# Head dimensions in neighbouring pairs across the partitions, fillers over the whole wait, a later planned landing

## The chip, the cores and the metric

The kernel runs on one core of a Trainium2 chip. The metric is device time in microseconds (us); the version before the change takes 1041.48 us, the median of three runs (1041.34 to 1042.71). Below, PE is the matrix engine (its weight loads are listed apart, as PEld), DVE the vector engine, ACT the scalar engine, POOL the GpSimd engine, and SP the engine whose queue issues the DMAs.

## What is computed

Four layers over a sequence of 2048 tokens of width 576 in bf16: attention, GLU, attention, GLU, each with a layer norm in front and a residual behind it. The two attention layers share their weights, and so do the two GLU layers.

```
x = x + A(layernorm(x))     # attention
x = x + B(layernorm(x))     # GLU
x = x + A(layernorm(x))
x = x + B(layernorm(x))

A: q, k, v = (x @ wqkv) as (3, 32 heads, 18 dims)
   logits[s, w] = q[s] . k[s - 2w] * 18**-0.5   for w = 0..7, -1e9 where s - 2w < 0
   o[s] = sum over w of softmax(logits)[s, w] * v[s - 2w];  return o @ wo
B: return ((x @ w_gate) * (x @ w_up)) @ w_down      # inner width 4608
```

Each token looks at eight earlier positions, two apart, in 32 heads of 18 dimensions. The attention is thus small products and sums on the vector engine, and nearly all matmul work is in the GLU.

## The kernel before, in words

**Tiles and stages.** The sequence is cut into tiles of 256 tokens (the first two of the first layer of 128). For each tile `attention` and then `glu` are called; j counts these stages. The sequence goes in two halves of eight 128-token blocks, each first through layer pair one and then through pair two. The GLU keeps its gate and up weights in SBUF and streams the down weights.

**The planner.** No call issues its work at once. Every piece is given to `Plan.op` (L48) with an engine, an assumed cost in ns, the names that it reads and writes, a priority and a rank (the stage, mostly; lower is more urgent). `Plan.run` (L109) keeps a clock for each engine, takes the piece that can begin first, and emits the pieces in that order. So the assumed costs and landing times decide the order of the instructions on each engine, and each engine then runs its own list strictly in order. For a DMA, the assumed end is a modelled transfer plus 2000 ns plus `late`. A piece of lower rank that would soon be ready holds back longer pieces of higher rank on its engine (L154 to L160).

**Fillers.** Until the first GLU piece, the planner puts dummy matmuls (L1207 to L1209, into an unused bank) into waits of PE. Their number is worked out at L176 to L179 from the gap between the clock of PE and the start of the next real piece. Pieces with a cost of zero, which emit nothing, move that clock too. One of them, at L884, holds a bank for the first gather until the attention weights have been spread.

**The head layout.** The weights arrive with columns ordered (head, dim), 18 dims to a head. The kernel copies them into `wqkv` with columns ordered (dim, head), so that after the projection the partitions of a 128-row block hold four dims of 32 heads: partition 32 * dim + head. The copies are made in `perm` (L388 to L418) for each of five 128-row slabs k, and for t3 = 0 (Q), 1 (K), 2 (V, in two halves), 3 (dims 16 and 17 of Q and K) and 4 (those of V). Each reads its source with a step of 18 elements. Q and the Q/K tails go to DVE; K goes to DVE for odd k and to ACT for even k; the V halves go to whichever of ACT and DVE the planner finds free first; the V tails go to ACT. The raw Q/K weights are loaded at L364 in six DMAs (slab 4 in two parts); the V loads wait until slab 2 of Q/K has landed.

**The first tile.** For j = 0 (`fast`) everything is ordered for a short chain: layer norm (L467 on), transposes of the normalised rows (L524), projection slab by slab as weights become ready (L606), products of q with the eight shifted k on DVE (L761), sums over the dims by the selector matrix `Esel` on PE (L776), softmax (L802 to L827), attention weights spread over the dims by the selectors `Bsel` (L842) and copied out of PSUM, products with v (L875), their sum by identity matmuls, the gathers (L879, L880), scaling (L902, L905), output projection (L940), residual (L910), the next layer norm, and the first GLU matmul (L993).

**Later tiles.** From j = 3 on, the attention weights are written to DRAM (L852) and read back by four DMAs (L855), one for each dim of four, each to 32 partitions. The first product with v (L875) waits for them. The planner assumes `late=1200` for these reads. GLU results are taken out of PSUM by ACT (L1028) and DVE (L1035), which frees the banks for PE.

## Time and profile before

| What | us |
|---|---|
| median of three runs | 1041.48 |
| lowest and highest run | 1041.34, 1042.71 |
| the profiled execution, in all | 1043.98 |
| its span, from first to last instruction | 1041.8 |
| PE busy in it | 1030.0 (99%) |
| DVE busy in it | 774.4 (74%) |
| ACT busy in it | 436.9 (42%) |

A page of the profile and answers about its trace are quoted below. In the windows by stage, each row is a stretch of time with its length, then the busy time of PE, PEld, DVE, ACT and POOL with the number of instructions, the granted PE clock (1.00 is full), the share of the DMA engines' time, and GB/s. In the order of time, a row has the start, how long the merged instructions lasted, engine, line, operation, what was written and read, the count, and in brackets the idle time just before with what ended it. In the rows grouped by line and form, busy time and the mean ns of one instruction stand behind the bar. In the waits, a row has the waiting engine and line, what it waited for, the us in total, the times, and the longest.

### The profile page before, as it was taken

Reading aid. Unit: us, or ns where it says so; the run is one execution under the profiler, and the core shown is the slowest. Engines: PE = TensorE matmul, PEld = TensorE weight load, DVE = VectorE, ACT = ScalarE, POOL = GpSimd, SP = SyncE. Lnnn points to the kernel's source line nnn. Section 1 sums busy time; section 2 is a strip of 40 time slices with the busy share of each in tenths; the row PEclk is TensorE's granted clock in tenths of the full one; section 3 lists DMA queues with packets and bytes.
Section 4 is the critical chain, followed back from the end, with each engine's and each line's share of the span. In section 5 each row is a group of like instructions: output and inputs, shape, how many; then the busy total and the mean of one; then the engine's idle time right before and its main releaser. Section 6 shows DMA issues by size and latency. Waiting matters only on the chain.

```text
span 1041.8 us, 40082 instructions
## 1 busy us (share of the span) xinstructions
PE 1030.0 (99%) x17899; PEld 813.5 (78%) x17899; DVE 774.4 (74%) x1450; ACT 436.9 (42%) x1169; POOL 8.9 (1%) x33
## 2 busy tenths in 40 slices
PE   7999999999999999999999999999999999999998
PEld 4788887778777787777779977877788778777776
DVE  8799786877768696877969597795977869574333
ACT  6644744354444654242343434434334333223231
POOL 3000000000000000000000000000000000000000
PEclk9999999999999999999999999999999999999999
DMA  9957333443443454433544426334443443343332
GB/s 278 336 183 219 110 90 112 134 101 102 108 145 89 100 116 108 130 103 95 151 130 106 108 72 154 104 83 109 106 131 92 111 124 117 97 147 86 123 97 70
DMA packets 144540, 129.66 MB, mean 124 GB/s; under 512 B 43440, under 2 KB 143728, under 8 KB 144368
## 3 DMA queue, kind: packets, MB, share of 16 engines
q1 hardware_dynamic: 144368, 127.10, 43.5%
q8 instruction: 140, 2.29, 0.9%
q14 instruction: 32, 0.26, 0.1%
HBM read 114.02 MB, written 4.19 MB: 113 GB/s over the span
## 4 chain that ended last, share of the span: by engine, by line
PE 92%; DVE 5%; DMA 1%; ACT 1%; issue 1%; POOL 0%; SPq 0%; DVEq 0%; POOLq 0%; ACTq 0%
PE pu L1017 19%; PE pg L1017 18%; PE pu L1086 10%; PE pa L1017 7%; PE acct L1017 6%; PE pg L1086 6%; PE pg L606 4%; PE pu L606 4%; PE pa L1086 3%; PE acct L1086 2%; PE pg L919 2%; PE pu L993 1%; PE pg L993 1%; DVE scr L875 1%; PE pg L1087 1%; DVE oT L897 1%
## 5 line engine op out<-in xcount | busy, mean ns | idle before, releaser
L1017 PEld LDWEIGHTS <-wg 64*128 64x128 bf16 x4320 | 392.6, 94 | 35.5 <-issue 1.7
L1017 PEld LDWEIGHTS <-wu 64*128 64x128 bf16 x4320 | 388.1, 94 | 27.7 <-ACT tok L550 0.2
L1017 PE MATMUL pg<-xnT_B,wg 64*128 64x256 bf16 x3168 | 407.7, 269 | 0.0
L1017 PE MATMUL pu<-xnT_B,wu 64*128 64x256 bf16 x3168 | 407.0, 269 | 0.4 <-DVE xf L1066 0.4
L1086 PE MATMUL pu<-wd,h 64*128 64x512 bf16 x792 | 203.4, 377 | 0.0
L1086 PE MATMUL pg<-wd,h 64*128 64x512 bf16 x792 | 203.3, 377 | 0.0
L1086 PEld LDWEIGHTS <-h 64*128 64x128 bf16 x2112 | 118.7, 94 | 106.9
L550 ACT COPY tok<-pu 1x1 f32<-1x1 f32 x289 | 42.6, 147 | 317.2 <-PE pu L1017 212.5
L1028 ACT CAST g_sb<-pg 128x512 bf16<-128x512 f32 x216 | 126.6, 588 | 94.0 <-PE pg L1017 81.4
L1035 DVE TENSOR_TENSOR h<-pu,g_sb 128x512 bf16<-128x512 f32 x169 | 115.6, 689 | 61.2 <-ACT g_sb L1028 60.3
L1087 PE MATMUL pu<-wd,h 64*128 64x64 bf16 x840 | 158.8, 189 | 0.0
L1087 PE MATMUL pg<-wd,h 64*128 64x64 bf16 x840 | 158.8, 189 | 0.0
L1017 PE MATMUL pa<-xnT_B,wu 64*128 64x256 bf16 x1152 | 156.8, 269 | 0.6 <-DVE h L1035 0.6
L1017 PE MATMUL acct<-xnT_B,wg 64*128 64x256 bf16 x1152 | 157.1, 269 | 0.0
L1087 PEld LDWEIGHTS <-h 64*128 64x128 bf16 x2112 | 116.1, 95 | 0.6
L606 PEld LDWEIGHTS <-wqkv 64*128 64x128 bf16 (+1 forms) x2030 | 99.5, 94 | 15.4 <-issue 1.5
L606 PE MATMUL pg<-xnT_A,wqkv 64*128 64x256 bf16 (+2 forms) x962 | 110.6, 265 | 0.2
L606 PE MATMUL pu<-xnT_A,wqkv 64*128 64x256 bf16 (+1 forms) x942 | 109.1, 266 | 0.6 <-DVE wqkv L408 0.4
L1017 PE MATMUL pg<-xnT_B,wgu_t 64*128 64x256 bf16 x396 | 106.5, 269 | 0.0
L1017 PE MATMUL pu<-xnT_B,wgu_t 64*128 64x256 bf16 x396 | 106.5, 269 | 0.0
L897 DVE TENSOR_TENSOR oT<-oT,scr 128x1280 bf16<-128x1280 bf16 (+1 forms) x112 | 89.8, 802 | 2.9
L784 DVE TENSOR_TENSOR scr<-qT,kv 128x1280 bf16<-128x1280 bf16 x112 | 88.0, 815 | 0.0
(185 smaller groups left out, 1546.3 us busy)
## 6 DMA issues: line engine op xcount, KB each, us to landing
wd<-in_B_w_down_dram SPq DMA_DIRECT2D x306, 288.0 KB, 4.4
scr<-a_dram SPq DMA_DIRECT2D x56, 128.0 KB, 2.6
wg<-in_B_w_gate_dram SPq DMA_DIRECT2D x6, 768.0 KB, 9.5
wu<-in_B_w_up_dram SPq DMA_DIRECT2D x6, 768.0 KB, 10.5
xb<-in_A_x_dram SPq DMA_DIRECT2D x7, 288.0 KB, 2.9
out_dram<-xf SPq DMA_DIRECT2D x14, 144.0 KB, 3.1
a_dram<-scr SPq DMA_DIRECT2D x14, 128.0 KB, 1.7
scr<-in_A_wqkv_dram SPq DMA_DIRECT2D x4, 288.0 KB, 3.7
```

The source lines that it names most:

```text
L550: box["at"] = nc.scalar.copy(tok[0:1, :], src())
L606: return nc.tensor.matmul(bank(p_, u)[0:m, e * n:(e + 1) * n], lhsT=wqkv[r_, k, w0:w0 + m], rhs=xnT_A[r_, k, c0:c0 + n], start=start, stop ...
L784: op("DVE", 70 + 2.6 * n, lambda p_=p_, e=e: nc.vector.tensor_tensor(late["prod"][p_ % 2][:, e, :, 0:n], qT[:, :, 0:n], kT[:, :, HALO - DI ...
L875: nc.vector.tensor_tensor(js(dst), js(vT[:, :, o0:o0 + n]), abw, op=ALU.mult)
L897: op("DVE", 70 + 2.63 * n, lambda i_=i_: nc.vector.tensor_tensor(oT[:, :, 0:n], oT[:, :, 0:n], late["prod"][i_ % 2][:, 0, :, 0:n], op=ALU. ...
L919: return nc.tensor.matmul(bank(hh, us[i])[:, 0:HD], lhsT=oT[rows, t, i * P:(i + 1) * P], rhs=wo_p[rows, t, hh * HD:(hh + 1) * HD], start=( ...
L993: nc.tensor.matmul(pt[:, e * n:(e + 1) * n], lhsT=w_[:, k, ft * P:(ft + 1) * P], rhs=xT[:, k, 0:n], start=(first and k == 0 and e == 0), s ...
L1017: return nc.tensor.matmul(ps[:, e * n:(e + 1) * n], lhsT=w_, rhs=xT[rows, k, 0:n], start=(first and e == 0 and k == 0), stop=(not first an ...
L1028: op("ACT", 490, lambda: nc.scalar.copy(g_sb[gs][:, 0:ul], pg[use["slot"]][:, 0:ul]), r=[f"wg_{j}_{u}"], w=[f"g{gs}"], prio=0, due=True)
L1035: op("DVE", 605, lambda: nc.vector.tensor_tensor(hb[hs][:, 0:ul], pu[use["slot"]][:, 0:ul], g_sb[gs][:, 0:ul], op=ALU.mult), r=[f"wu_{j}_{ ...
L1086: return [lambda: nc.tensor.matmul((pg, pu)[i][use["slot"]][:], lhsT=lhs, rhs=wt[rows, e % 2, 0:512], start=first, stop=fin, skip_group_ch ...
L1087: lambda: nc.tensor.matmul((pg, pu)[i][tl["slot"]][:, 0:TL], lhsT=lhs, rhs=wt[rows, e % 2, 512:D], start=first, stop=fin, skip_group_check ...
```

## The change

The head dimensions are laid on the partitions in neighbouring pairs: within a 128-row block the partition is now 64 * (dim // 2) + 2 * head + dim % 2, where it was 32 * dim + head. The copies of `perm` then read and write runs of two elements. Everything that knows the layout follows: `Esel`, `Bsel`, the load of the output weights, and the four reads of the spread attention weights, whose destinations now step two partitions. All K copies go to DVE. The costs that the planner assumes for the copies are lower, the ranks of the copies change, and each part of the raw Q/K weights gets its own planned landing (`LAND`) instead of 700 for each. The number of fillers is worked out from `real`, the end of the last PE piece with a cost, instead of from the clock of PE. The planned landing of the spread's reads goes from `late=1200` to `late=2000`.

```diff
-VP = ["ACT"] * 5
-VT = ["ACT"] * 5
+LAND = (290, 420, 600, 970, 1400, 1500)
...
+        real = 0.0
...
-                    each = 430 if clock["PE"] < 5500 else 215
-                    n = int((t - max(clock["PE"], 900) - 150) * 0.75 / each)
+                    each = 430 if real < 5500 else 215
+                    n = int((t - max(real, 900) - 150) * 0.75 / each)
...
+            if o.eng == "PE" and o.cost:
+                real = o.end
...
-    Bsel = sb("Bsel", [P, 4, 4, 32])
+    Bsel = sb("Bsel", [P, 4, 2, 32, 2])
...
-                   nbytes=rows * (c1 - c0) * 2, prio=1 + (c == "b"), late=700 if c == "a" else 0)
+                   nbytes=rows * (c1 - c0) * 2, prio=1 + (c == "b"), late=LAND[k + (r_ > 0)] if c == "a" else 0)
...
-                    src = wr.rearrange("p (h d) -> p d h", h=H)[:, 0:16, :]
-                    dst = wqkv[:, k, t3 * 512:(t3 + 1) * 512].rearrange("p (d h) -> p d h", h=H)
+                    src = wr.rearrange("p (h d e) -> p d h e", h=H, e=2)[:, 0:8]
+                    dst = wqkv[:, k, t3 * 512:(t3 + 1) * 512].rearrange("p (d h e) -> p d h e", h=H, e=2)
...
-                    src = (wrawa, wrawb)[t3 - 3][:, k, :].rearrange("p (t h d) -> p t d h", t=t1 - t0, h=H)[:, :, 16:18, :]
-                    dst = wqkv[:, k, 3 * 512:3 * D].rearrange("p (t d h) -> p t d h", t=3, h=H)[:, t0:t1]
+                    src = (wrawa, wrawb)[t3 - 3][:, k, :].rearrange("p (t h d) -> p t h d", t=t1 - t0, h=H)[:, :, :, 16:18]
+                    dst = wqkv[:, k, 3 * 512:3 * D].rearrange("p (t h e) -> p t h e", t=3, h=H)[:, t0:t1]
...
-                pl.rank = 0.5
+                pl.rank = 0 if k + t3 == 0 else 0.5 if t3 in (0, 1, 3) else 0.7
...
-                            f(dst[:, 8 * hf:8 * hf + 8], src[:, 8 * hf:8 * hf + 8])
-                        box["o"] = op("ACT", 565, half, r=rk, w=[f"{key}{'ab'[hf]}"], prio=3, alts={"DVE": 320, "ACT": 565})
+                            f(dst[:, 4 * hf:4 * hf + 4], src[:, 4 * hf:4 * hf + 4])
+                        box["o"] = op("ACT", 450, half, r=rk, w=[f"{key}{'ab'[hf]}"], prio=3, alts={"DVE": 190, "ACT": 450})
...
-            perm("DVE", 530, f"wq0_{k}", 0, ra)
-            perm("DVE", 180, f"wq3_{k}", 3, ra)
-            if k % 2:
-                perm("DVE", 530, f"wq1_{k}", 1, ra)
-            else:
-                perm("ACT", 1000, f"wq1_{k}", 1, ra)
-            perm(VP[k], {"ACT": 1050, "DVE": 560, "POOL": 1250}[VP[k]], f"wq2_{k}", 2, rb)
-            perm(VT[k], {"ACT": 330, "DVE": 200, "POOL": 300}[VT[k]], f"wq4_{k}", 4, rb)
+            perm("DVE", 280, f"wq0_{k}", 0, ra)
+            perm("DVE", 280, f"wq1_{k}", 1, ra)
+            perm("DVE", 150, f"wq3_{k}", 3, ra)
+            perm("ACT", 450, f"wq2_{k}", 2, rb)
+            perm("ACT", 300, f"wq4_{k}", 4, rb)
...
-                                        fill=1.0, base=-32 * j, pattern=[[-1, 32]], channel_multiplier=1)
+                                        fill=1.0, base=-64 * (j // 2) - j % 2, pattern=[[-2, 32]], channel_multiplier=1)
...
-                                        base=-32 * j, pattern=[[0, 4], [-1, 32]], channel_multiplier=1)
+                                        base=-32 * j, pattern=[[0, 2], [-1, 32], [0, 2]], channel_multiplier=1)
...
-            op("SP", 470, dma(wo_p[32 * dd:32 * dd + 32, 0:KF, :], wv_[:, dd:16:4, :]), w=[f"wo{dd}"], nbytes=32 * KF * D * 2, prio=2.6)
+            op("SP", 470, dma(wo_p[64 * (dd // 2) + dd % 2:64 * (dd // 2) + 64:2, 0:KF, :], wv_[:, dd:16:4, :]), w=[f"wo{dd}"], nbytes=32 * KF * D * 2, prio=2.6)
...
-                op("SP", 600, lambda g=g: nc.sync.dma_start(late["ab"][32 * g:32 * g + 32, :, 0:W * sq],
+                op("SP", 600, lambda g=g: nc.sync.dma_start(late["ab"][64 * (g // 2) + g % 2:64 * (g // 2) + 64:2, :, 0:W * sq],
                                                             dr[:, 0:W * sq].rearrange("(j h) n -> h j n", j=4)),
-                   r=[f"adr{j % 2}", "ab"], w=[f"ab{g}"], prio=0, nbytes=P * W * sq * 2, late=1200)
+                   r=[f"adr{j % 2}", "ab"], w=[f"ab{g}"], prio=0, nbytes=P * W * sq * 2, late=2000)
```

Three other lines follow the new shape of `Bsel` and of the two last rows of the output weights in the same way.

More of the change, by code (lines that the diff above doesn't have):

```diff
@@ L841, in spread @@
                     for e in range(nb):
-                        nc.tensor.matmul(b()[:, e * W * sq:(e + 1) * W * sq], lhsT=Bsel[:, j0 + e].rearrange("p a b -> p (a b)"),
+                        nc.tensor.matmul(b()[:, e * W * sq:(e + 1) * W * sq], lhsT=Bsel[:, j0 + e].rearrange("p a b c -> p (a b c)"),
                                          rhs=late["a_c"][:, 0:W * sq], start=(e == 0), stop=(e == nb - 1), skip_group_check=True)
```

4 lines of the change are left out of this document (2 added, 2 removed).

## The prediction

> **What bounds the kernel now.** I read the page's first part, then the windows by stage, then what the matrix engine (PE) waited for.
>
> ```profile
> span 1041.8 us, 40082 instructions
> PE 1030.0 (99%) x17899; PEld 813.5 (78%) x17899; DVE 774.4 (74%) x1450; ACT 436.9 (42%) x1169; POOL 8.9 (1%) x33
> ```
>
> ```profile
> 40.00:100.00 60.00, 59.69 (x933) 50.23 (x933) 52.23 (x107) 32.21 (x74) 0.00 (x0) 1.00 0.75 224
> 100.00:1000.00 900.00, 899.02 (x15909) 710.50 (x15905) 675.50 (x1237) 370.06 (x1016) 0.00 (x0) 1.00 0.41 112
> 1000.00:1042.00 42.00, 38.62 (x627) 30.15 (x622) 13.23 (x24) 9.09 (x26) 0.00 (x0) 1.00 0.27 86
> ```
>
> ```profile
> PE pu L879 <- DVE scr L875: 2.0, 1, 2.0
> PE pa L1017 <- DVE h L1035: 0.6, 1, 0.6
> PE pu L1017 <- DVE xf L1066: 0.4, 1, 0.4
> ```
>
> From 40 to 1000 us PE idles 1.3 us in 960; the idle after 1038.6 is the last output leaving. The changed lines shorten no PE instruction, and the reordered partitions leave every operand's shape as it is, so a gain can come only from the start, before the first GLU matmul at 31.18 us. There the order of time shows one serial chain:
>
> ```profile
> 4.85 5.55 DVE L408 COPY wqkv<-scr 128x512 bf16<-128x512 bf16 x12
> 10.30 0.69 DVE L405 COPY wqkv<-scr 128x256 bf16<-128x256 bf16 x2
> 12.13 3.03 DVE L761 TENSOR_TENSOR scr<-qT,kv 128x1280 bf16<-128x1280 bf16 x4
> 15.08 0.68 DVE L405 COPY wqkv<-scr 128x256 bf16<-128x256 bf16 x2
> 15.79 0.42 DVE L802 TENSOR_REDUCE mx<-pu 128x32 f32<-128x256 f32 x1
> 19.42 0.89 DVE L875 TENSOR_TENSOR scr<-kv,scr 128x640 bf16<-128x640 bf16 x2
> 19.97 0.38 PE L879 MATMUL pu<-scr,ident 128*128 128x512 bf16 x1 [1.98 <-DVE scr L875]
> 24.87 0.75 DVE L902 TENSOR_TENSOR oT<-pu,rzs 128x256 bf16<-128x256 f32 x2 [0.76 <-PE pg L880]
> 31.18 1.21 PE L993 MATMUL pg<-xnT_B,wg 128*128 128x128 bf16 x16 [0.57 <-ACT xnT_B L531]
> ```
>
> Q and K weight copies, projection, products, softmax, values, gathering, output projection, then the GLU. PE is fed by DVE all along it. What this chain loses, the whole run loses, because PE has no idle time behind it in which to catch up.
>
> **The change, part by part.** *The copies.* Their present prices:
>
> ```profile
> L408 DVE COPY wqkv<-scr x12: 273/614/884, 4.8 to 10.1; 128x512 bf16<-128x512 bf16 x7, 128x128 bf16<-128x128 bf16 x5
> L405 DVE COPY wqkv<-scr 128x256 bf16<-128x256 bf16 x4 | 1.4, 390 | 0.0
> L405 ACT COPY wqkv<-scr 128x256 bf16<-128x256 bf16 x6 | 3.7, 660 | 0.0
> L408 ACT COPY wqkv<-scr 128x512 bf16<-128x512 bf16 x3 | 3.3, 1114 | 0.1
> L408 ACT COPY wqkv<-scr 128x64 bf16<-128x64 bf16 x5 | 1.5, 313 | 0.0
> L591 ACT COPY kv<-halo 128x140 bf16<-128x140 bf16 x3 | 0.9, 303 | 2.0 <-POOL halo L384 2.0
> ```
>
> On ACT the strided source costs (1114-660)/256 = 1.77 ns an element over a fixed 207 ns; the dense copy of 140 elements costs only (303-207)/140 = 0.69. The jump from element to element is what is paid. On DVE, (614-390)/256 = 0.88 ns over a fixed 166. In runs of two there are half the jumps. Priced by run, a 512-element DVE copy costs what 256 jumps cost now, 0.39 us; priced by element it stays at 0.61. A V half on ACT lies between 0.43 and 0.66, a 128-element tail on DVE between 0.22 and 0.28. I take the lower ends, because the dense row shows that it is the jump which costs. Two copies in a row took 0.69 us, so the next one starts 0.30 behind the last.
>
> DVE now gets 15 copies rather than 12: the three K copies that ACT made move over. Twelve of them (k = 0 to 3) take 8 x 0.30 + 4 x 0.14 = about 3.0 us. They are not the limit any more; what is late next is the last slab:
>
> ```profile
> 3.09 1.20 SPq L364 DMA_DIRECT2D scr<-in_A_wqkv_dram  x2
> scr<-in_A_wqkv_dram SPq DMA_DIRECT2D x2, 144.0 KB, 4.8
> 8.56 0.22 issue
> 8.78 1.44 DVE wqkv L408 x3
> ```
>
> Its second issue is at about 3.7, and lands 4.8 later, at 8.5; the chain shows it waiting there already, 0.22 us between two DVE copies. From 8.6, three copies end at 8.6 + 0.30 + 0.30 + 0.22 = 9.4 instead of 10.40: **-1.0 us**, at best -1.1, at worst -0.3 if the twelve copies run late. The first copy is put ahead of the small bias instruction at 4.77, on which ACT's xn and PE's transposes hang; DVE idles 0.73 us there, which hides its 0.39, and without that cover xn, and PE's projection with it, would be up to 0.4 late. ACT, rid of 3 x 1.1 us, is free when V lands. All ten V halves on ACT would take about 10 x 0.33 + 5 x 0.2 = 4.3 us (0.1 of each overlaps the next). Placed from 11.0 they end at 15.3, beside the products and ahead of the 15.76 of now. The two halves on DVE at 15.08 hold the maximum back by at most 0.2; I count nothing for that.
>
> *The fillers.* They were counted from a clock that a zero-cost placeholder (L884) moves forward. Now they are counted from the last real PE instruction. Only the wait before the first gather (19.97, idle 1.98) has such a placeholder in it. Planned wait 1.6 to 2.4 us: (1600-150) x 0.75 / 215 = 5 to (2400-150) x 0.75 / 215 = 7 fillers, 1.1 to 1.5 us, where one stands. Queued behind them are the gather and the transposes for the next tile, and DVE's last product waits for a buffer that the gathers free; they would suffer only if the real wait were under 1.5 us. What they are worth:
>
> ```profile
> 4.03:7.45 3.42, 1.99 (x12) 0.74 (x11) 2.69 (x8) 3.16 (x7) 3.30 (x9) 1.00 1.02 333
> 14.28:17.69 3.41, 2.81 (x62) 1.92 (x62) 3.34 (x9) 2.32 (x7) 0.00 (x0) 1.00 1.06 278
> 17.69:21.10 3.41, 1.43 (x16) 0.66 (x14) 3.31 (x11) 2.51 (x7) 0.00 (x0) 1.00 1.08 338
> 21.10:24.51 3.41, 3.38 (x17) 1.63 (x16) 2.52 (x7) 1.15 (x3) 0.00 (x0) 0.50 1.06 332
> 20.84 0.38 PE L879 MATMUL pu<-scr,ident 128*128 128x512 bf16 x1
> 21.35 0.60 PE L524 MATMUL pa<-ident,xn 128*128 128x128 bf16 x4
> 22.13 0.61 PE L879 MATMUL pu<-scr,ident 128*128 128x512 bf16 x1
> 22.64 0.63 PE L879 MATMUL pu<-scr,ident 128*128 128x512 bf16 x1
> 22.88 0.49 DVE L875 TENSOR_TENSOR scr<-kv,scr 128x640 bf16<-128x640 bf16 x1 [0.48 <-PE pg L880]
> ```
>
> A stretch with PE busy for 1.43 of 3.41 us (42%) is followed by one at half the granted clock; after 58% busy it is not. In the slow stretch gathers go out 0.51 to 0.53 us apart and the last product waits 0.48 for its buffer. At full clock: transposes from 21.35 take 0.39, gathers 4 to 7 go at 0.27 from 21.74, the last product runs from 22.31 to 22.80, its gather ends at 23.25, and L902 starts at 23.4 and not at 24.87: **-1.45 us**. The fillers lift the 1.43 to at least 2.3 of 3.41. Bounds: 0 and -1.5.
>
> The Trainium skill ("TensorE: Matmul & The Clock Gate", section "Why this matters for your kernels") says that PE idle gaps up to about 3 us are safe, so by it a 1.98 us wait would not cool the clock and this term would be nothing, the sum -1.0. The trace disagrees: the clock stood at 0.50 behind a gap of that length, so the measurement decides.
>
> *The spread.* Its planned landing moves from 1200 to 2000 in 14 stages.
>
> ```profile
> DVE oT L875 <- DMA scr<-a_dram: 29.6, 12, 5.5
> 540.78 0.82 DVE L875 TENSOR_TENSOR oT<-kv,scr 128x1280 bf16<-128x1280 bf16 x1 [1.43 <-DMA scr<-a_dram]
> 547.90 0.68 DVE L1035 TENSOR_TENSOR h<-pa,g_sb 128x512 bf16<-128x512 f32 x1
> ```
>
> DVE waits 2.5 us on average for it, with GLU evacuations queued behind; only once did that reach PE (L1035 at 547.90, the 0.6 above). PE at 899.02 of 900 hides the rest. Between -1.2 (all of PE's late waits go) and +1.2 (as many new ones); I take 0.
>
> *At nothing:* the DMAs that now step two partitions move as many runs of the same length; output weights are issued by 13 us and needed at 25.7. The selectors on POOL are as many, and end before 10 while the products come at 11 at the earliest. The first GLU weights do not bind: PE waits for xnT_B at 31.18, not for a DMA.
>
> Sum: -1.0 - 1.45 = -2.45, say -2.5 us. The profiled execution took 1043.98 in all around its span of 1041.8, 2.5 over the runs' median; the difference goes to the median: 1041.48 - 2.5 = **1039.0**.
>
> **The rivals.** *The clock falls all the same* (or would not have fallen): only the copies count, -1.0, 1040.4. For it: where the stretches begin is set by nothing in the program. Against: 2.3 of 3.41 us is 67%, well over the 58% that kept the clock. The page's rule on idle gaps leads here too.
>
> *The copies do not get shorter.* Then 10 x 0.61 + 5 x 0.25 = 7.3 us on DVE from 4.85: end at 12.2, +1.8, with the clock -1.45: 1041.8. For it: nothing in the trace has runs of two. A lock would do the same:
>
> ```profile
> 5.00:10.00 5.00, 3.69 (x46) 2.72 (x46) 5.00 (x11) 4.86 (x7) 4.75 (x17) 1.00 1.02 294
> ```
>
> POOL is busy 4.75 of these 5 us, and the longest DVE copy (884) is 0.27 over the median. If each of the 12 early copies paid 0.27, they would end at 4.85 + 3.0 + 3.2 = 11.1 and the three behind them at 11.9. The Trainium skill ("SBUF — State Buffer", section "Who interferes with whom") has such a rule: a DVE copy that reads through two ports and a GpSimd instruction shut each other out for a whole instruction. The median at 614 beside POOL says that it is not paid each time.
>
> *Slower: the value chain blocks the evacuations.* The products that now begin 0.8 us later by plan run ahead of waiting GLU evacuations, as at 540.78 to 547.90, in stage after stage. A block cost PE 0.6; in all 14 stages +8.4 - 2.5 = +5.9, 1047.4. It eats the gain from 5 stages on and is over 0.2% slower from 8. For it: DVE is busy 52.2 of 60 us early on. Against: it happened once in 14.
>
> *More:* PE's late waits go too, -3.7, 1037.8.
>
> **How the numbers follow.** Forecast 0.57 (own range 1038.2 to 1040.0), clock 0.14, copies 0.09, blocked evacuations 0.15, more 0.05. About 0.2%, 2.1 us, is what a measurement of this kernel tells from no change, to 1039.4: of the forecast 0.50 lies beyond it, so faster 0.55; within it 0.07 + 0.14 + 0.09 = 0.30; slower 0.15. The range reaches from "more" over the two near rivals, 1037.4 to 1042.0, and leaves out the blocked evacuations.
>
> **What would show it.** Copies: 128x512 on DVE near 390 ns, the last ending near 9.4, products from about 11.0. Clock: no stretch at 0.50 between 17 and 25 us, several L1209 ahead of the first L879, L902 near 22.3. First GLU matmul near 28.7. Spread: PE still over 99% busy from 40 us on. It is wrong if the first GLU matmul does not move by 2 us, or if it does and PE's idle time behind 40 us grows by as much.

## The result and the profile after

The changed kernel takes 1044.28 us (median of 21 runs, 1043.64 to 1045.16); the kernel before took 1043.09 us beside it (21 runs, 1041.16 to 1044.57). The ratio is 1.0012, with a 95% interval of 1.0006 to 1.0017: about 1.2 us slower, where 2.5 us faster was forecast. The profiled execution took 1044.3 us. One run each of two experiments below (e9 and e11) took over 3300 us and is left out of their ratios.

The kernel before is not at 1041.48: that was the median of three runs, and the median of 21 is 1043.09. Its runs come in groups by the granted clock of PE. Of the 35 runs beside e16 below, 10 had a mean clock of 1.000 and took 1041.3 to 1042.1 us, 14 had 0.998 and took 1042.3 to 1044.1, and 11 had 0.997 and took 1043.8 to 1044.9. One stretch of 3.41 us at half clock lowers the mean over 1042 us by 0.0016, as in the profiled execution of before (0.998, 1043.98 us); two lower it by 0.0033.

All line numbers in this section are those of the changed kernel: one less than before from about L420 on, and 2 more around L335 to L410, so that the products are L760, the values L874, the gathers L878, the scaling L901, the first GLU matmul L992, the fillers L1208, the Q/K copies L410 and the V halves L407.

First the page, then the windows by stage (columns as before):

```profile
span 1042.5 us, 40131 instructions
PE 1031.6 (99%) x17907; PEld 819.4 (79%) x17907; DVE 774.8 (74%) x1454; ACT 432.4 (41%) x1165; POOL 9.5 (1%) x33
```

```profile
4.10:7.52 3.42, 1.79 (x15) 0.81 (x14) 2.74 (x8) 2.17 (x5) 3.30 (x8) 1.00 0.99 293
7.52:10.93 3.41, 3.41 (x36) 3.41 (x34) 3.16 (x11) 0.84 (x4) 2.84 (x13) 0.50 0.83 240
...
17.76:21.17 3.41, 2.50 (x13) 1.17 (x12) 3.31 (x11) 1.44 (x4) 0.00 (x0) 1.00 1.05 384
21.17:24.58 3.41, 3.31 (x33) 1.89 (x33) 3.38 (x10) 1.88 (x4) 0.00 (x0) 1.00 1.08 314
...
100.00:1000.00 900.00, 899.10 (x15907) 714.90 (x15904) 676.28 (x1238) 370.61 (x1016) 0.00 (x0) 1.00 0.41 112
```

Behind 100 us PE is as busy as it was (899.10 of 900, before 899.02). The half-clock stretch at 21 to 24.5 us is gone, as forecast: PE is now busy for 2.50 of the 3.41 us ahead of it (73%, before 42%). But there is a new one at 7.52 to 10.93, behind a stretch with PE busy for 1.79 us (52%); in the kernel before that stretch had 1.99 (58%) and the clock stayed full.

The order of time up to the first GLU matmul:

```profile
4.01 0.39 DVE L410 COPY wqkv<-scr 128x512 bf16<-128x512 bf16 x1
4.86 0.93 DVE L410 COPY wqkv<-scr 128x512 bf16<-128x512 bf16 x2
6.09 3.73 DVE L410 COPY wqkv<-scr 128x512 bf16<-128x512 bf16 x9 [0.30 <-DMA scr<-in_A_wqkv_dram]
10.07 0.27 DVE L407 COPY wqkv<-scr 128x256 bf16<-128x256 bf16 x1 [0.25 <-DMA scr<-in_A_wqkv_dram]
10.26 0.80 DVE L410 COPY wqkv<-scr 128x512 bf16<-128x512 bf16 x3
10.98 0.81 DVE L407 COPY wqkv<-scr 128x256 bf16<-128x256 bf16 x4
11.88 0.69 DVE L687 CAST kv<-pu 128x512 bf16<-128x512 f32 x1
12.65 0.81 PE L1208 MATMUL acct<-g_sb 128*128 128x512 bf16 x3
13.15 0.29 DVE L687 CAST kv<-pu 64x128 bf16<-64x128 f32 x1 [0.58 <-ACT qT L716]
13.55 3.03 DVE L760 TENSOR_TENSOR scr<-qT,kv 128x1280 bf16<-128x1280 bf16 x4
18.84 1.67 PE L1208 MATMUL acct<-g_sb 128*128 128x512 bf16 x7
20.65 0.89 DVE L874 TENSOR_TENSOR scr<-kv,scr 128x640 bf16<-128x640 bf16 x2
21.20 0.38 PE L878 MATMUL pu<-scr,ident 128*128 128x512 bf16 x1 [0.68 <-DVE scr L874]
24.66 0.76 DVE L901 TENSOR_TENSOR oT<-pu,rzs 128x256 bf16<-128x256 f32 x2
30.53 0.29 DVE L532 COPY xnT_B<-pu 128x256 bf16<-128x256 bf16 x1 [0.32 <-PE pu L525]
30.86 0.48 ACT L530 COPY xnT_B<-pu 128x384 bf16<-128x384 bf16 x1 [0.51 <-DVE xnT_B L532]
31.39 0.83 PE L992 MATMUL pg<-xnT_B,wg 128*128 128x128 bf16 x12 [0.90 <-ACT xnT_B L530]
```

Read it against the rows of before, link by link. The last Q/K copy ends at 11.06 (10.40 before), and the first product follows 2.49 us behind it (1.73 before): +1.42. From the values to L901 it takes 4.01 us (5.45 before), with seven fillers ahead of the first gather: -1.44. From L901 to the GLU it takes 6.73 (6.31 before): +0.42, of which 0.33 stands in the idle time at L992 (0.90 for 0.57), where the two parts of `xnT_B` now come in the other order. The links between add -0.2. The sum is +0.21: 31.39 for 31.18. Behind the GLU's start, PE needs 1007.71 us to its end (1007.45 before), and the last output leaves 3.43 us after that (3.14 before). The profiled execution of before lies 0.9 us above its median, so these differences do not add up to the 1.2 us of the runs.

Against the forecast, the copies are 1.66 us late (11.06 for 9.4). Slab 4 landed at 9.41, where its copies were to begin at 8.6, which is 0.8; the copies of slabs 0 to 3 ended at 9.82, another 0.4; and a V half that stood in front and waited for its load let slab 4's copies begin at 10.26, the last 0.4. The first product was to follow 1.6 us behind the copies and follows 2.49: two fillers stand on PE ahead of slab 4's matmuls, which begin at 11.42, and V products stand ahead of the tails, so that ACT copies the tail of q only at 12.85.

Why the copies ended no earlier is seen in the groups by line and form, changed kernel first, the kernel before below it:

```profile
L410 DVE COPY wqkv<-scr 128x512 bf16<-128x512 bf16 x10 | 3.9, 424 | 0.3 <-DMA scr<-in_A_wqkv_dram 0.3
L410 DVE COPY wqkv<-scr 128x128 bf16<-128x128 bf16 x5 | 3.0, 593 | 0.0
L407 DVE COPY wqkv<-scr 128x256 bf16<-128x256 bf16 x5 | 1.1, 266 | 0.3 <-DMA scr<-in_A_wqkv_dram 0.3
L407 ACT COPY wqkv<-scr 128x256 bf16<-128x256 bf16 x5 | 1.8, 414 | 2.9 <-DMA scr<-in_A_wqkv_dram 2.9
...
L425 POOL TENSOR_SCALAR_AFFINE_SELECT Bsel<-Bsel 128x128 bf16<-128x128 bf16 x4 | 3.3, 821 | 0.0
```

```profile
L408 DVE COPY wqkv<-scr 128x512 bf16<-128x512 bf16 x7 | 4.7, 692 | 0.0
L408 DVE COPY wqkv<-scr 128x128 bf16<-128x128 bf16 x5 | 1.6, 319 | 0.0
...
L426 POOL TENSOR_SCALAR_AFFINE_SELECT Bsel<-Bsel 128x128 bf16<-128x128 bf16 x4 | 2.1, 530 | 0.0
```

The large copies are nearly as short as forecast (424 on average). The small ones, a quarter of their size, have become longer than the large ones: 593 ns. POOL's selects for `Bsel` have become longer too. The shortest and the longest of the Q/K copies lie far apart (min, median and max in ns):

```profile
L410 DVE COPY wqkv<-scr x15: 204/394/714, 4.0 to 10.9; 128x512 bf16<-128x512 bf16 x10, 128x128 bf16<-128x128 bf16 x5
```

### The profile page after: what moved, and what is told of

It reads as the page before. It is cut to its first block, busy times and chain, and to the rows that moved or that the text cites. A ratio compares the mean times of both kernels' runs of the same rounds, so it can differ in the third digit from the quotient of the medians.

```text
span 1042.5 us, 40131 instructions
## 1 busy us (share of the span) xinstructions
PE 1031.6 (99%) x17907; PEld 819.4 (79%) x17907; DVE 774.8 (74%) x1454; ACT 432.4 (41%) x1165; POOL 9.5 (1%) x33
## 4 chain that ended last, share of the span: by engine, by line
PE 95%; DVE 4%; ACT 1%; POOL 0%; issue 0%; POOLq 0%; ACTq 0%; DVEq 0%
PE pu L1016 19%; PE pg L1016 18%; PE pu L1085 8%; PE pa L1016 7%; PE pg L1085 6%; PE acct L1016 6%; PE pa L1085 4%; PE pg L605 4%; PE acct L1085 4%; PE pu L605 3%; PE pg L918 2%; PE pu L992 1%; PE pg L992 1%; PE pg L1086 1%; PE acct L605 1%; PE pu L1086 1%
## 5 line engine op out<-in xcount | busy, mean ns | idle before, releaser
L1085 PEld LDWEIGHTS <-h 64*128 64x128 bf16 x2112 | 122.1, 94 | 102.9 <-issue 1.1
L1086 PE MATMUL pg<-wd,h 64*128 64x64 bf16 x960 | 181.4, 189 | 0.0
L1086 PE MATMUL pu<-wd,h 64*128 64x64 bf16 x960 | 181.4, 189 | 0.0
L1085 PE MATMUL pu<-wd,h 64*128 64x512 bf16 x672 | 173.8, 377 | 0.0
L1085 PE MATMUL pg<-wd,h 64*128 64x512 bf16 x672 | 173.7, 377 | 0.0
L1016 PE MATMUL acct<-xnT_B,wg 64*128 64x256 bf16 x1120 | 152.5, 269 | 0.0
L1086 PEld LDWEIGHTS <-h 64*128 64x128 bf16 x2112 | 119.9, 95 | 0.7
L1085 PE MATMUL pa<-wd,h 64*128 64x512 bf16 x384 | 99.3, 377 | 0.0
L1085 PE MATMUL acct<-wd,h 64*128 64x512 bf16 x384 | 99.2, 377 | 0.0
L605 PE MATMUL pg<-xnT_A,wqkv 64*128 64x256 bf16 (+2 forms) x809 | 95.1, 266 | 0.2 <-ACT xnT_A L535 0.2
L605 PE MATMUL pu<-xnT_A,wqkv 64*128 64x256 bf16 (+1 forms) x789 | 94.5, 268 | 0.1
```

What stands on the lines that cost most here:

```text
L605: return nc.tensor.matmul(bank(p_, u)[0:m, e * n:(e + 1) * n], lhsT=wqkv[r_, k, w0:w0 + m], rhs=xnT_A[r_, k, c0:c0 + n], start=start, stop ...
L1016: return nc.tensor.matmul(ps[:, e * n:(e + 1) * n], lhsT=w_, rhs=xT[rows, k, 0:n], start=(first and e == 0 and k == 0), stop=(not first an ...
L1085: return [lambda: nc.tensor.matmul((pg, pu)[i][use["slot"]][:], lhsT=lhs, rhs=wt[rows, e % 2, 0:512], start=first, stop=fin, skip_group_ch ...
L1086: lambda: nc.tensor.matmul((pg, pu)[i][tl["slot"]][:, 0:TL], lhsT=lhs, rhs=wt[rows, e % 2, 512:D], start=first, stop=fin, skip_group_check ...
```

## The experiments

Theory A: the chain before the first product is longer, because DVE's copies and POOL's selects shut each other out, and because V work whose load has not landed stands ahead of Q/K work. Theory B: the new half-clock stretch costs it. Theory C: the start differs with the landing of the loads in each execution, and the change itself does little. Where an edit is not shown in full, the rest of it only serves the lines shown.

### The parts alone: e1, e2, e3

e1 is the kernel before with the filler count alone:

```diff
-                    n = int((t - max(clock["PE"], 900) - 150) * 0.75 / each)
+                    n = int((t - max(real, 900) - 150) * 0.75 / each)
```

> The kernel before with the new count of the fillers alone. If the fillers are worth what the prediction gave them, no stretch at half clock lies between 17 and 25 us, the first scaling (L902) comes 1.4 us earlier than 24.87 and the run is 1.4 us faster, ratio 0.9987. The other view, that the half clock at 21.10 was an accident of where the activity stretches began in that execution, expects a median within 0.4 us of before, because most runs of before would not have the slow stretch at that place.

Measured: 0.9984 [0.9975, 0.9992]. The order of time of e1 (there L905 is the scaling, L996 the first GLU matmul):

```profile
23.48 0.74 DVE L905 TENSOR_TENSOR oT<-pu,rzs 128x256 bf16<-128x256 f32 x2
29.78 1.21 PE L996 MATMUL pg<-xnT_B,wg 128*128 128x128 bf16 x16 [0.57 <-ACT xnT_B L534]
```

The scaling stands at 23.48, where 23.4 was forecast, and the GLU starts 1.40 us earlier. The filler term holds at the start. Behind the GLU's start PE needs 1006.19 us, 1.26 less than in the trace of before, of which 1.0 is late waits that are gone; how much of the runs' gain is this, the runs do not tell.

e2 is the kernel before with the later planned landing alone:

```diff
-                   r=[f"adr{j % 2}", "ab"], w=[f"ab{g}"], prio=0, nbytes=P * W * sq * 2, late=1200)
+                   r=[f"adr{j % 2}", "ab"], w=[f"ab{g}"], prio=0, nbytes=P * W * sq * 2, late=2000)
```

> The kernel before with the planned landing of the spread at 2000 instead of 1200, alone. The prediction gave it 0, between -1.2 and +1.2: ratio 0.9989 to 1.0011, start unchanged (first GLU matmul at 31.2). If it is what costs the changed kernel its 1.2 us, the ratio is near 1.0012 and new waits of PE of 0.5 us or more stand behind 40 us.

Measured: 1.0002 [0.9994, 1.0011]. PE's waits behind 35 us in e2:

```profile
PE pa L1087 <- DVE h L1035: 0.8, 1, 0.8
PE pu L606 <- ACT tok L550: 0.3, 1, 0.3
```

A wait of 0.8 takes the place of 0.6 and 0.4. It only moved: zero, as forecast.

e3 is the changed kernel with these two edits taken back, so it holds the layout, the copies, their ranks and `LAND`:

```diff
-                    n = int((t - max(real, 900) - 150) * 0.75 / each)
+                    n = int((t - max(clock["PE"], 900) - 150) * 0.75 / each)
...
-                   r=[f"adr{j % 2}", "ab"], w=[f"ab{g}"], prio=0, nbytes=P * W * sq * 2, late=2000)
+                   r=[f"adr{j % 2}", "ab"], w=[f"ab{g}"], prio=0, nbytes=P * W * sq * 2, late=1200)
```

> The changed kernel with the old count of the fillers and the old planned landing of the spread: layout, copies, ranks and the landings of the loads alone. Theory A (the chain before the products is longer: copies held up by POOL, V copies and V matmuls put ahead of what the chain waits for): first product near 13.5 as in the changed kernel, against 12.13, and a run 1.2 to 2.6 us slower than before. Rival C (the loads merely landed a microsecond late in the profiled execution): the V loads are issued near 6.1 here, the first product is near 12.4, and the run is not over 1 us slower.

Measured: 1.0020 [1.0011, 1.0029], so +2.1 us. The product comes at 13.02, between the two views. Yet the GLU starts at 31.19, no later than before: in this execution the loss stands behind the GLU's start, where PE needs 1009.83 us (1007.45 before). Of these 2.4 us, 1.4 are longer waits of PE, the longest 1.2 us for DVE's `h` at 550 us. With -1.7 for e1 and +0.2 for e2 the parts add to +0.6 us, against 1.2 [0.6, 1.8] for the whole. The layout part, meant as -1.0, is what turned the sign, but not by the start alone.

### One cause undone at a time: e4 to e7

e4 orders the V halves behind the last Q/K copy (the V tails are only listed after the Q/K copies):

```diff
-                        box["o"] = op("ACT", 450, half, r=rk, w=[f"{key}{'ab'[hf]}"], prio=3, alts={"DVE": 190, "ACT": 450})
+                        box["o"] = op("ACT", 450, half, r=rk, w=[f"{key}{'ab'[hf]}"], prio=3, alts={"DVE": 190, "ACT": 450}, after=lastqk)
```

> The changed kernel with all V copies ordered behind the last Q/K copy. Theory A: the three copies of slab 4 no longer stand behind a V copy that waits for its load, so they end 0.4 us earlier than 11.06 or at the landing of slab 4 plus 0.9, and the run is 0.3 to 0.8 us faster than the changed kernel's 1044.3. Rival B (the half clock from 7.5 to 10.9, which makes the projection's matmuls late, sets the products): no gain, as PE is not ready earlier.

Measured: 1.0000 [0.9991, 1.0009]. In its profiled execution the first copy waited for its load until 5.30, the last ended at 10.49, and the copies of q and k out of PSUM waited for PE until 13.26 (product at 14.69). PE ran at half rate up to about 12 us there, as shown below e7.

e5 keeps POOL quieter: of its zeros, only those that are needed first are written early, and the others wait for the last Q/K copy, so that the selects are done sooner.

```diff
+            i = nc.gpsimd.memset(qT_[1][TL:P, KF, :], 0.0)
+            tc.add_manual_dep(i.ins, held["c"].ins.name, sync)
```

> The changed kernel with POOL kept quiet during the copies: only the zeros that the first tile needs are written ahead of the selectors, and the others wait for the last Q/K copy. Theory A (DVE copies and POOL instructions shut each other out): 128x512 copies near 385 ns throughout instead of a third of them at 630 to 715, the twelve copies of slabs 0 to 3 done in 3.2 to 3.6 us instead of 5.1 to 5.8, and the run 0.5 to 1.2 us faster than the changed kernel's 1044.3. The rival, that runs of two cost DVE by the element now and then (source lines, not POOL), leaves the long copies where they are and the run at 1044.

Measured: 1.0012 [1.0004, 1.0021], no change where 0.5 to 1.2 us was expected, though in the profiled execution the copies of slabs 0 to 3 ended at 8.70 (9.82 in the changed kernel) and the product came at 12.46. The last three Q/K copies stand behind a V half that waits for its load until 9.40.

e6 puts the tails of q and k out of PSUM ahead of the V products:

```diff
                     key = (ka, kb)[part]
+                    if part:
+                        o = evac(ua, ka, ea, False) or o
+                        o = evac(ub, kb, eb, True) or o
```

> The changed kernel with the copies of the q and k tails out of PSUM emitted ahead of the V matmuls. Theory A: these copies wait for the V matmuls in front of them (11.80 to 12.85 in the changed kernel), so the first product comes 0.5 to 1.0 us earlier, measured from the end of the last Q/K copy (2.5 us behind it in the changed kernel), and the run is 0.4 to 1.0 us faster than 1044.3. Rival B (the half clock during the projection is the cost): no gain from it.

Measured: 1.0013 [1.0005, 1.0021], no gain where 0.4 to 1.0 us was expected; product at 12.96, GLU at 31.02.

e7 puts more fillers into PE's first wait, for theory B:

```diff
-                    n = int((t - max(real, 900) - 150) * 0.75 / each)
+                    n = int((t - max(real, 900) - 150) * (1.2 if real == 0 else 0.75) / each)
```

> The changed kernel with more fillers in the first wait of PE (factor 1.2 instead of 0.75 there, about 13 instead of 8). Rival B: no half clock behind 7.5 us, projection matmuls at full rate, and the run 0.5 to 1 us faster than 1044.3. Theory A: the projection waits for the copies and the V matmuls anyway; the gain is under 0.3 us.

Measured: 1.0009 [1.0000, 1.0018]. No half clock at 7.5 us, but one later; the windows of e7:

```profile
15.97:19.38 3.41, 3.08 (x24) 1.49 (x11) 3.05 (x10) 1.42 (x4) 0.00 (x0) 0.50 1.04 380
12.56:15.97 3.41, 1.96 (x92) 1.52 (x91) 3.31 (x5) 2.15 (x7) 0.00 (x0) 1.00 0.94 197
```

Of these four, only e4 has its middle outside the changed kernel's interval, and the two intervals overlap. The runs show no gain from any of the others alone. The middle of e7 gives back 0.3 us, with a half clock of its own later, so B alone is not shown to be the cause.

The traces give theory B more weight than that, though. In them the record of the granted clock begins with the first stretch at full clock. Ahead of it the matmuls run at half rate, and the windows show 1.00 there all the same. The rate is seen in the time of five projection matmuls, the first row from the half-clock stretch of the changed kernel, the second from the kernel before at full clock:

```profile
10.31 0.74 PE L605 MATMUL pu<-xnT_A,wqkv 128*128 128x128 bf16 x5
7.70 0.44 PE L606 MATMUL pu<-xnT_A,wqkv 128*128 128x128 bf16 x5
```

By this measure PE was at half rate up to about 12 us in e4 and e10, 10 in e6 and e9, and 9 in e3 and e12. The first product comes at 14.69, 14.66, 12.96, 12.78, 13.02 and 12.50 there, and at 13.55 in the changed kernel. In the eleven traces with full rate during the projection it comes at 11.35 to 12.66. Of the seven traces of the new layout without e7's fillers, six are slowed in this way; of the six with them, none. This puts part of the late product on the clock, though no run changes the clock alone, and the trace of the changed kernel does not say how much is the order.

### V behind everything: e8, e9, e10

e8 joins e4 to e7.

> POOL kept quiet, tails first, more early fillers, and V copies behind the last Q/K copy, all in the changed kernel. Theory A and B together: Q/K copies end at the landing of slab 4 plus 0.9 (9.4 to 10.4), first product 1.5 us behind them (11.0 to 12.0), no half clock, first GLU matmul near 28.7 to 29.7, run at 1040.0 to 1041.7, ratio to before 0.997 to 0.9985. If the loads of one execution decide (rival C), the first product is not ahead of 12.1.

Measured: 1.0005 [0.9993, 1.0017], short of what A and B together expected. The Q/K copies end at 9.86, but ACT's copy of q out of PSUM starts only at 11.18, behind two V tails for whose loads ACT waits.

e9 is the changed kernel with every V copy, tails too and on both engines, ordered behind the copies of q and k out of PSUM:

```diff
+                        for v in vcopy:
+                            v.order.add(o)
```

> The changed kernel, with every copy of a V column block (halves and tails, on both engines) ordered behind the copies of q and k out of PSUM (main parts). Theory A (the chain before the first product is longer because V work whose load has not landed stands ahead of Q/K work): slab 4's three copies follow their landing at once, the last Q/K copy ends at 10.4 or earlier (11.06 in the changed kernel), the copies of q and k start within 0.5 us of it, the first product at 12.3 to 12.7 (13.55). The V chain is then 1 to 2 us later, so that the first weighted value (20.65) gains less than the products: the first GLU matmul at 30.3 to 31.0, ratio 0.9990 to 1.0005. Rival (only the lock with POOL's work sets it, and V's place does not matter): product at 13.2 to 13.6, GLU at 31.2 to 31.5, ratio 1.001 or more. Rival (V is the tighter chain): product earlier, but the weighted values at 20.6 or later, and the GLU matmul no earlier.

Measured: 0.9991 [0.9982, 1.0000]; product at 12.78, GLU at 30.36. The GLU and the ratio are within what A expected, and outside both rivals. But A did not have all of it: the last Q/K copy ends at 10.06, and the copies of q and k, which were to start within 0.5 us of it, wait for PE:

```profile
11.64 1.04 DVE L696 CAST kv<-pu 128x512 bf16<-128x512 f32 x2 [1.58 <-PE pu L609]
```

This one edit moves the ratio by 0.0021, more than the change as a whole did. In the traces 1.03 us of it stand ahead of the GLU and 0.55 behind its start (1007.16 for 1007.71). The V chain does not take over: the first weighted value comes at 20.02.

e10 puts ACT's part of the first `xnT_B` ahead of DVE's again:

```diff
-                   prio=prio, **b.drop())
+                   prio=prio, after=oa, **b.drop())
```

> The changed kernel, with ACT's part of the first xnT_B ordered ahead of DVE's part, as it stood before the change. If the flipped order costs what the trace shows, PE's gap ahead of the first GLU matmul goes from 0.90 back to about 0.57 us: 0.3 us, ratio 1.0009 (changed kernel 1.0012). If the order costs nothing, the gap stays at 0.9 and the ratio at 1.0012. The two ratios are closer than the intervals; the gap in the trace tells them apart.

Measured: 1.0008 [0.9999, 1.0017]. The gap at the GLU in e10:

```profile
32.16 1.05 PE L992 MATMUL pg<-xnT_B,wg 128*128 128x128 bf16 x13 [0.57 <-ACT xnT_B L530]
```

0.57 again, so the order does cost 0.33 us there. (The GLU is late because this is a trace at half rate up to 12 us.) The ratio can't tell so little apart.

### Everything undone: e11, with e12 as a yardstick

e11 is the changed kernel with the edits of e5, e6, e7, e9 and e10.

> The changed kernel with everything that theory A names undone at once: POOL's later zeros behind the last Q/K copy, V copies behind the copies of q and k out of PSUM, tails of q and k ahead of the V products, ACT's part of xnT_B first, and more fillers in the first wait. Theory A: the Q/K copies end within 1.0 us of slab 4's landing, at 9.4 to 10.0, the first product at 11.2 to 11.8, the first GLU matmul at 29.0 to 29.9, the run 1040 to 1041.5, ratio 0.997 to 0.9985: then the short copies are worth what was forecast once nothing stands in their way. Rival (the V chain takes over): products at 11.2 to 11.8, but the weighted values at 20 or later and the GLU matmul at 30.4 or later, ratio 1.000 or more, and the short copies are worth nothing in this kernel. Rival (landing of the loads differs by execution and sets the start anyhow): product at 12.3 or later with the copies waiting for their loads.

Measured: 0.9991 [0.9982, 1.0000]. Its order of time, then its groups by line and form up to 7.2 us and after it:

```profile
4.31 0.50 DVE L406 COPY wqkv<-scr 128x512 bf16<-128x512 bf16 x1 [0.45 <-DMA scr<-in_A_wqkv_dram]
4.81 2.63 DVE L406 COPY wqkv<-scr 128x512 bf16<-128x512 bf16 x8
7.62 0.81 DVE L406 COPY wqkv<-scr 128x512 bf16<-128x512 bf16 x3 [0.17 <-DMA scr<-in_A_wqkv_dram]
8.92 0.82 DVE L406 COPY wqkv<-scr 128x512 bf16<-128x512 bf16 x3 [0.48 <-DMA scr<-in_A_wqkv_dram]
11.35 3.03 DVE L786 TENSOR_TENSOR scr<-qT,kv 128x1280 bf16<-128x1280 bf16 x4
28.92 1.21 PE L1018 MATMUL pg<-xnT_B,wg 128*128 128x128 bf16 x16 [0.57 <-ACT xnT_B L539]
```

```profile
L406 DVE COPY wqkv<-scr 128x512 bf16<-128x512 bf16 x6 | 2.4, 429 | 0.4 <-DMA scr<-in_A_wqkv_dram 0.4
L406 DVE COPY wqkv<-scr 128x128 bf16<-128x128 bf16 x2 | 1.4, 707 | 0.0
...
L406 DVE COPY wqkv<-scr 128x512 bf16<-128x512 bf16 x5 | 1.7, 383 | 0.7 <-DMA scr<-in_A_wqkv_dram 0.7
L406 DVE COPY wqkv<-scr 128x128 bf16<-128x128 bf16 x3 | 0.6, 208 | 0.0
```

While POOL's selects run (to 6.85), a small copy takes 707 ns; behind them, with POOL idle or at its short memsets, the same copy takes 208. The copies now wait for their loads, as forecast (the last three from 8.92; forecast 8.6), and the GLU starts at 28.92 (forecast 28.7). But the run gains less than half of that, and stays outside the 0.997 to 0.9985 that A expected. What PE waited for in e11:

```profile
PE pa L1112 <- DVE h L1060: 0.8, 1, 0.8
PE pg L1074 <- DMA wd<-in_B_w_down_dram: 0.8, 1, 0.8
```

The second is new: some 9 us behind the GLU's start PE comes to the second group of three down weights, and is ahead of their load.

e12 is the kernel before with the filler count and the tails first, in the old layout.

> The kernel before with the filler count of the change and with the tails of q and k ahead of the V products, old layout. Fillers alone gave 0.9984. If the tails gain what they gained in the changed kernel's trace (product 13.55 to 12.96), product at 11.6 to 11.9 and the first GLU matmul at 29.2 to 29.5, ratio 0.9978 to 0.9982. If the product's time is set by the Q/K copies alone here (1.7 us behind the last one), 12.1, 29.8 and 0.9984. It is also the yardstick for the run above: whether the old layout with these two does as well as the new one with everything in its place.

Measured: 0.9989 [0.9980, 0.9998]; product at 12.50, GLU at 30.15, both later than either view expected. The tails are worth nothing there, and the new layout with everything in its place is no better than the old one with the fillers.

### What eats the rest: e13 to e16

e13 is e11 with the planned landing of the spread back at 1200.

> The kernel with everything undone (e11), with the spread's planned landing back at 1200 ns. If the later landing is what puts DVE's h 0.8 us late at 389 us (that wait stood in every trace with 2000 and in none with 1200), it goes, others of the kind at 548 and 860 us may come (0.0 to 1.0 us in all in the traces with 1200 and the old layout), and the run is 0.0 to 0.8 us shorter: ratio 0.9983 to 0.9993. If the wait only moves, as in the forecast, the sum of the late waits stays at 0.8 to 1.3 us and the ratio at 0.9991.

Measured: 0.9991 [0.9983, 1.0000]; the 0.8 at L1112 is gone, 0.4 and 0.2 elsewhere came for it, and the wait for the down weights stays, at 0.9. The runs show no gain.

e14 is e11 with the second three down weights issued ahead of the third slab of gate and up weights:

```diff
-           late=0 if first else 0, prio=5.5 + (i // 3 if first else 0))
+           late=0 if first else 0, prio=5.5 + (i // 6 if first else 0))
```

> The kernel with everything undone (e11), with the second group of three down weights issued ahead of the third slab of gate and up weights. In e11 the GLU started 2.3 us earlier than before the change, but TensorE then waited 0.8 us for that group. If only the order of the issues is at fault, this wait goes, no other takes its place, and the run is 0.8 us shorter (0.9983). If the DMA engines, busy at 99 per cent from 12 us on, set it, TensorE waits for the third slab of gate and up weights instead, by 0.5 us or more, and the ratio stays at 0.999 or rises: then a GLU started ahead of about 29.7 us gains nothing in this kernel.

Measured: 0.9986 [0.9977, 0.9994]; GLU at 29.45, no wait for weights at 38 us, and none for the third slab. (The trace names the down weights at the GLU's own first wait; it is the same 0.57 that is put down to `xnT_B` elsewhere.)

e15 has both edits.

> Both edits of the two runs above. If both waits go away, 0.9975 to 0.9983, which would be the forecast's gain in full; if neither does, 0.999 or more.

Measured: 0.9986 [0.9978, 0.9995]; GLU at 29.33. Behind the GLU's start PE has two waits left, both for DVE's `xf`, of 0.3 and 0.2 us.

e16 repeats e1.

> The kernel before with the filler count alone, a second time, as a yardstick on the same chip for the three above. Expected 0.998 to 0.999 with a GLU start of 29.6 to 30.2 us. If the short copies are worth anything once nothing stands in their way, the runs above lie below it by 0.0005 or more; if the loads of the weights cap the gain, they lie within 0.0005 of it.

Measured: 0.9988 [0.9979, 0.9996]; GLU at 29.77. So the order of the loads was at fault for the wait at 38 us, not the DMA engines' capacity: e14 took it away and no other wait for a load came for it, while e13, whose GLU starts later (29.60), still has it. Still e14 and e15 lie within 0.0005 of the fillers alone. e15's GLU starts 0.44 us ahead of e16's, yet its PE ends at 1036.67 and e16's at 1036.19. From the first GLU matmul to its end PE takes 1007.34 us in e15 and 1006.42 in e16, and only 0.15 of that 0.92 is a difference in late waits. The same matmuls (17,603 in both traces) run in another order. Why that order takes 0.8 us longer was not settled.

The same split runs through all the traces. From the first GLU matmul to its end PE takes 1006.0 to 1006.4 us in the three of the old layout with the fillers (e1, e12, e16), 1007.5 and 1007.2 in the two without (before, e2), and 1007.2 to 1009.8 in all thirteen of the new layout. So against the old layout with the fillers the new one loses 0.7 us or more behind the start, whatever is done at the start, and no run shows which of its parts does it.

## Why the prediction was wrong

**The copies (-1.0): wrong in sign, and the step that turned the forecast.** The prices were right: 383 ns for a 128x512 copy with POOL idle (e11, behind POOL's selects; 0.39 forecast), 414 for a V half on ACT (0.43 to 0.66). The step that failed is "From 8.6, three copies end at 9.4", and the products from 11.0 behind it: the copies ended at 11.06 and the products began at 13.55. Three things failed in it.

First, "twelve of them take about 3.0 us. They are not the limit any more." They took from 4.86 to 9.82 for eleven of the twelve. The small third copy of each of these slabs waited out an instruction of POOL, mostly a select for `Bsel`: 593 ns on average and 714 at most, 208 behind POOL's selects in e11. The lock is not all of it: slab 3 itself landed only at 8.42 (7.33 before), and three copies from there would end at 9.24. The rival had the lock, at 0.27 a copy; it was some 0.5 on one copy in three. It was kept small because the median of before, 614, "beside POOL says that it is not paid each time". That median belongs to another pattern: it said nothing of copies in runs of two. It was also misread. It is the middle of twelve copies of two sizes; of the seven large ones 610 and 617 are the shortest, and the other five took 642 to 884. And the lock alone did not turn the sign: in e5 the twelve copies ended at 8.70, and the runs did not gain.

Second, "the selectors on POOL are as many, and end before 10". They are as many, but the pattern with three parts takes 821 ns on average where the one with two took 530, 1.2 us more in all. (The selects for `Esel` fell from 1.9 to 1.1 us, so the selects as a whole grew by 0.4; but a longer instruction is a longer lock.)

Third, "all ten V halves ... placed from 11.0" was my placing and not the planner's. It put one V half on DVE ahead of slab 4's Q/K copies, where it waited for its load until 10.07 with them queued behind it, four more ahead of the copy of k out of PSUM (these cost nothing in this trace: they ended at 11.79, and the copy waited for PE until 11.88), and V products and fillers on PE ahead of the tails of q and k. The prediction worked with durations and let the order look after itself; the lower planned costs, ranks and landing times changed just that order. Of the single edits, e9, which undoes the order of V, gives back the most, 0.0021 of the ratio, and is the only one with a middle below 1. How the order acts was not separated: in e9's own trace the copies of q and k waited for PE. Two other things had a share in the trace of the changed kernel: PE's half clock during the projection, and the loads, as slab 4 landed 5.8 us behind its issue (4.8 before).

**The fillers (-1.45): right in mechanism and size.** No half clock from 17 to 25 us, PE busy 2.50 of 3.41 (at least 2.3 forecast), and alone 1.7 us [0.8, 2.6] and 1.3 [0.4, 2.2] shorter than before (e1, e16). All 11 runs of e16 had a mean clock of 1.000 and took 1041.2 to 1042.1, just what the 10 runs of before with that clock took. The new stretch at 7.52 was not foreseen: `xnT_A` now comes earlier, and two fillers stand there where four stood. e7 shows that it can be filled; what it costs in the runs was not told apart from the order of V.

**The base (1041.48): wrong by 1.6 us.** "The difference goes to the median" took the 2.5 us between the profiled execution and the median of three runs as fixed. But the profiled execution had the half-clock stretch that the fillers were to remove, and two of the three runs (1041.34, 1041.48) took no longer than runs of before without one. From them this term could not be gained: the rival "would not have fallen" holds for such runs. It was the luck of three runs. From 1043.09 the same sum would have given 1040.6; of the 5.3 us between 1039.0 and 1044.28, 1.6 are the base and 3.7 the sum.

**The spread (0): right as far as it was run.** Alone 1.0002; with everything else undone, 1200 and 2000 give the same ratio, twice. Fillers and the later landing in the old layout were not run together.

**"A gain can come only from the start":** PE's time behind the first GLU matmul was taken as fixed. It was not: 1007.71 us in the changed kernel and 1006.19 in e1, which has the same fillers. Of the 3.4 us between these two traces 1.6 stand ahead of the GLU's start, 1.5 behind it and 0.3 behind PE's end.

**"What this chain loses, the whole run loses":** not shown of a gain either. e11 started the GLU 2.26 us before the old kernel and PE ended 1.85 earlier; the next limit was the load of the down weights, which "at nothing" had not looked at: it asked only whether the first gate and up weights bind at 31.18, not what binds at 28.7.

**The rivals.** The nearest was that the copies get no shorter, with a lock, at 1041.8. Evacuations blocked by the value chain did not come in stage after stage: PE idled 0.9 us in 900, as before. (e3 had one such block of 1.2 us, at 550.) No rival had the order of V or PE's time behind the start in it. The slowdown of 1.2 us lies within the 2.1 us that counted as no change; the time lies above the range because of the base and the copies together.

## What to carry to other kernels

When a list of instructions comes out of a planner, a cheaper operation is first of all another order: ask which instruction will now stand ahead of a wait, and whose load has not landed. Before a gain at the start is carried to the end, find the load that is needed next and see how long it lands ahead of its use. Take the base from many runs, and ask which of the terms a quick run already has: three runs put it 1.6 us too low here. And of a change with several parts, measure each part alone: here one line of it, the filler count, gives 0.9984 in the old kernel, and nothing that was run beats it by more than the interval.

## What the runs showed of the hardware

A DVE copy in runs of two and a POOL select shut each other out for a whole instruction: a small copy takes 707 ns beside POOL's selects and 208 behind them, in one trace (e11). The Trainium skill ("SBUF — State Buffer", section "Who interferes with whom") says that a copy in a two-port mode and a GpSimd instruction fully block each other; the trace agrees. In which mode the copies ran, no run shows.

POOL's select over a pattern of three parts, [[0, 2], [-1, 32], [0, 2]], takes twice what the shortest over two parts takes for the same 128x128 elements, with no copy in its way. In the order of time of e11:

```profile
3.11 0.71 POOL L423 TENSOR_SCALAR_AFFINE_SELECT Bsel<-Bsel 128x128 bf16<-128x128 bf16 x1
```

and of the kernel before, beside DVE's copies even (one more of the four took 0.36 there, and the other two 0.71):

```profile
5.77 0.35 POOL L426 TENSOR_SCALAR_AFFINE_SELECT Bsel<-Bsel 128x128 bf16<-128x128 bf16 x1
```

The clock has no sharp share of busy time in these numbers: PE busy 1.99 of 3.42 us kept it full in the kernel before, 1.96 of 3.41 in e7 (above) was followed by 0.50, and so was 2.02 in e3, whose windows read

```profile
16.04:19.45 3.41, 3.35 (x29) 1.63 (x29) 3.08 (x10) 1.27 (x5) 0.00 (x0) 0.50 1.02 367
12.63:16.04 3.41, 2.02 (x73) 1.38 (x72) 3.31 (x6) 2.18 (x7) 0.00 (x0) 1.00 0.96 187
```

The Trainium skill ("TensorE: Matmul & The Clock Gate", section "Why this matters for your kernels") allows idle gaps of about 3 us; here shorter ones were enough when there were several in a stretch: 1.38 and 0.25 us in the changed kernel ahead of 7.52, 0.97 and 0.41 in e7 ahead of 15.97.

The same load (slab 4 of Q/K, the median of its two parts), issued at the same time, landed 4.8, 5.8 and 5.1 us after its issue in three traces (before, changed, e11). Over all traces its second part landed at 8.5 to 8.8 us in the five of the old layout and at 8.7 to 9.5 in the thirteen of the new; whether the new layout makes it late is not shown. Single executions of this kernel thus differ at the start by about 1 us, and a trace is only compared with another link by link.
